# The first batch's later queries: scores from rounded query and key halves instead of full float32

## The chip, the cores and the metric

The kernel runs on one core of one Trainium2 chip. The metric is the device time of one execution in microseconds (us), as the median of several runs; every view of the profile is of one profiled execution of the same program.

## The reference, cut to what matters

```python
scores = 1/sqrt(64) * q @ k.T                     # 8 batches, 8 heads, 576 x 576, head size 64
scores = where(scores >= rowmax(scores) - tau, scores, -1e9)
attn = exp(scores - rowmax(scores)); attn /= attn.sum(-1) + 1e-9
x = (attn @ v) -> (4608, 512)                     # heads side by side, one row per query
h = x @ w_in                                      # (4608, 2048)
out = (s * relu(h)**2 + b) @ w_out                # (4608, 512)
```

The weights come as float64 and are made into float32 on the chip.

## The kernel before, in words

**Tiles.** A tile is 128 queries of one head (or 64 leftover queries of each of two heads, a tail tile) against all 576 keys. For each tile TensorE makes the scores (`s`, line L356, in the PSUM bank `s` or `o`), VectorE takes them out with the row maximum (`sm`, L359), ScalarE makes the exponential (`em`, L365), VectorE masks it and sums it (L368), GpSimd divides (L376), TensorE transposes (`tp` and `tt`, L385 and L386), ScalarE takes the transposes out, and TensorE multiplies with the values (`pv`, L404 or L436). `sm` and `em` have two buffers each.

**Two kinds of attention.** Batch 0 (the first 36 tiles, numbered 0 to 35 here) is plain: its pair of heads lies in one buffer, k in 128 rows (64 of each head), q the same, v beside them (class `Plain`), and the products are in plain float32. From batch 1 on, a head is split (class `Head`): k is loaded twice, into both halves of the 128 partitions of `rk`, and q into `rq`; ScalarE rounds k to the rounded type fp32r (L306), GpSimd makes the rest, k minus its rounded copy (L307), ScalarE rounds q (L314), and VectorE puts the rest of q into the lower 64 rows (L315). One tile's scores are then four fp32r products (two halves of the keys times rounded k and rest of k) over 128 rows, where a plain tile has two float32 products over 64 rows, or over 128 for a tail tile, whose stationary operand `qd` holds the tails of both heads. `rk`, `rq` and `rv` are single buffers.

**Visits.** Each batch is gone through in two halves of queries; a visit is one pair of heads in one half. Batch 0 has tiles 0 to 15 in its first half (four per pair) and tiles 16 to 35 in its second (five per pair, the tail tile third). Tiles 0 to 15 use the banks `s` and `o` in turn, later ones only `s`.

**The feed-forward part** goes over blocks of 256 rows of x: for each of 16 slices f of the 2048 hidden columns, 12 products into bank `h` (L567), relu, square and rounding on ScalarE, a rest `gl` on GpSimd (L577), and 6 products into bank `o` (L583). The weights of a slice are loaded on SyncE's queue (L462 and L465), converted by ScalarE and VectorE (L497 to L508), and stay in the buffer `w0` to `w15`. Block 0 (the first half of batch 0) is worked on while the second half's tiles run, as far as its slices are converted. `xl` (L553) is the rest of its x.

**Borrowed room.** In batch 0 the four pairs lie in buffers that later serve other things: pair 0 in `w15`, pair 1 in `v`, pair 2 in `k`, pair 3 in `e`. A function `split_buffers` hands `e`, `k` and `v` over to the split heads of batch 1.

**The order.** Every operation is entered in a planner (`Plan`) with engine, assumed cost, keys read and written, and a due time; the planner lists them and the result is the fixed order on every engine. Each engine works through its own list in order, so an instruction that waits holds up all behind it. SyncE's list is all the loads.

## Time and profile before

| | |
|---|---|
| runs | 1365.67, 1367.85 and 1368.5 us, median 1367.85 |
| span of the profiled execution | 1365.4 us |
| its own time | not listed by itself; the fastest run stands 0.27 us above the span, the median 2.45 us above |
| TensorE (PE) busy | 1349.2 us, 99% of the span |
| VectorE (DVE) / ScalarE (ACT) / GpSimd (POOL) busy | 1082.1 / 989.4 / 762.3 us |
| granted TensorE clock, mean | 0.997 |
| batch 0's scores on PE | 5.9 us to about 146 us |

How to read it: "busy" is the time in which an engine had an instruction in work; PE matmuls overlap, so their durations are longer than the distance from start to start, and it is the distances that add up to time. In rows of groups the two numbers after the bar are busy us and mean ns of one. In rows of stretches each engine has its busy us and the number of instructions, and then come the granted PE clock, the busy share of the DMA engines and GB/s. In the rows in order of time, the first two columns are the start and the duration in us.

### The profile page before, as it was taken

Reading aid. Unit: us, or ns where it says so; the run is one execution under the profiler, and the core shown is the slowest. Engines: PE = TensorE matmul, PEld = TensorE weight load, DVE = VectorE, ACT = ScalarE, POOL = GpSimd, SP = SyncE. Lnnn points to the kernel's source line nnn. Section 1 sums busy time; section 2 is a strip of 40 time slices with the busy share of each in tenths; the row PEclk is TensorE's granted clock in tenths of the full one; section 3 lists DMA queues with packets and bytes.
Section 4 is the critical chain, followed back from the end, with each engine's and each line's share of the span. In section 5 each row is a group of like instructions: output and inputs, shape, how many; then the busy total and the mean of one; then the engine's idle time right before and its main releaser. Section 6 shows DMA issues by size and latency. Waiting matters only on the chain.

```text
span 1365.4 us, 29419 instructions
## 1 busy us (share of the span) xinstructions
PE 1349.2 (99%) x9369; PEld 1230.8 (90%) x9369; DVE 1082.1 (79%) x3097; ACT 989.4 (72%) x2467; POOL 762.3 (56%) x800
## 2 busy tenths in 40 slices
PE   9899999999999999999999999999999999999998
PEld 6677799998999999999999999999999999999897
DVE  7977789989888888888888888888788888887111
ACT  5787677777777777777777777777777677776443
POOL 2334466665766566655666566655666566664210
PEclk9999999999999999999999999999999999999999
DMA  9530122222222222222222222222222212220000
GB/s 317 206 98 16 37 74 73 85 56 70 77 88 63 62 79 74 77 63 60 71 82 61 72 57 82 72 72 56 61 79 68 75 51 73 67 77 15 17 16 16
DMA packets 94539, 99.59 MB, mean 73 GB/s; under 512 B 34480, under 2 KB 72368, under 8 KB 94384
## 3 DMA queue, kind: packets, MB, share of 16 engines
q1 hardware_dynamic: 94384, 97.71, 24.0%
q8 instruction: 74, 1.21, 0.4%
q14 instruction: 81, 0.66, 0.2%
HBM read 88.21 MB, written 9.44 MB: 72 GB/s over the span
## 4 chain that ended last, share of the span: by engine, by line
PE 93%; DVE 2%; issue 1%; ACT 1%; POOL 0%; DVEq 0%; POOLq 0%; ACTq 0%
PE h L567 30%; PE o L583 29%; PE s L356 12%; PE pv L436 10%; PE tp L385 9%; PE tt L386 2%; PE pv L404 1%; DVE em L368 1%; PE h L519 1%; DVE sm L359 0%; POOL em L376 0%; ACT em L365 0%; DVE e L423 0%; DVE w L508 0%; DVE oo L594 0%
## 5 line engine op out<-in xcount | busy, mean ns | idle before, releaser
L567 PE MATMUL h<-xh,w 128*128 128x256 f32 x2304 | 466.0, 285 | 0.0
L376 POOL TENSOR_SCALAR em<-em,st 128x576 f32<-128x576 f32 x288 | 263.2, 914 | 230.4 <-DVE st L373 137.2
L567 PEld LDWEIGHTS h<-xh,w 128*128 128x128 f32 x2304 | 376.6, 190 | 10.2 <-ACT g L573 1.0
L583 PE MATMUL o<-w,gh 128*128 128x512 f32 x1152 | 371.1, 403 | 0.1
L577 POOL TENSOR_TENSOR gl<-g,gh 128x256 fp32r<-128x256 f32 x272 | 225.7, 830 | 245.8 <-ACT gh L576 94.3
L567 PE MATMUL h<-xl,w 128*128 128x256 f32 x1152 | 325.5, 283 | 0.0
L368 DVE SCALAR_TENSOR_TENSOR em<-sm,st,em 128x577 f32<-128x577 f32 x288 | 273.4, 950 | 13.2 <-ACT em L365 6.6
L365 ACT ACTIVATE em<-sm,st 128x576 f32<-128x576 f32 x288 | 225.1, 781 | 36.2 <-DVE sm L359 18.7
L359 DVE TENSOR_SCALAR_CACHE_REDUCE sm<-s 128x576 f32<-128x576 f32 x280 | 210.9, 753 | 47.3 <-PE s L356 36.4
L573 ACT ACTIVATE g<-h 128x256 f32<-128x256 f32 x288 | 109.9, 381 | 181.6 <-PE h L567 175.3
L583 PE MATMUL o<-w,gl 128*128 128x512 f32 x576 | 226.6, 393 | 0.0
L423 DVE TENSOR_TENSOR e<-tp,e 128x512 fp32r<-128x512 f32 (+1 forms) x280 | 177.7, 635 | 60.2 <-ACT e L420 56.9
L567 PEld LDWEIGHTS h<-xl,w 128*128 128x128 f32 x1152 | 219.2, 190 | 6.2 <-DVE xl L553 0.2
L583 PEld LDWEIGHTS o<-w,gh 128*128 128x128 f32 x1152 | 195.1, 190 | 22.8 <-issue 2.1
L307 POOL TENSOR_TENSOR k<-rk,k 128x576 fp32r<-128x576 f32 x112 | 175.0, 1562 | 59.1 <-ACT k L306 57.0
L420 ACT CAST e<-tp 128x512 fp32r<-128x512 f32 (+1 forms) x280 | 150.7, 538 | 43.7 <-PE tp L385 39.8
L385 PE MATMUL tp<-ident,em 128*128 128x128 f32 x1152 | 174.4, 274 | 3.6 <-POOL em L376 3.2
L356 PE MATMUL s<-k,q 128*128 128x288 f32 x896 | 163.2, 304 | 1.4 <-DVE sm L359 1.4
L385 PEld LDWEIGHTS tp<-ident,em 128*128 128x128 f32 x1152 | 137.7, 140 | 25.5 <-issue 6.1
L436 PE MATMUL pv<-e,v 128*128 128x320 f32 (+1 forms) x1008 | 153.5, 297 | 0.2 <-DVE e L423 0.2
L436 PEld LDWEIGHTS pv<-e,v 128*128 128x128 f32 x1008 | 141.7, 190 | 3.9 <-DVE e L423 1.1
L356 PEld LDWEIGHTS s<-k,q 128*128 128x128 f32 x896 | 132.2, 190 | 7.8 <-DVE sm L359 2.5
(109 smaller groups left out, 1783.3 us busy)
## 6 DMA issues: line engine op xcount, KB each, us to landing
rk<-in_k_dram SPq DMA_DIRECT2D x224, 144.0 KB, 2.7
rv<-in_v_dram SPq DMA_DIRECT2D x112, 128.0 KB, 2.1
rq<-in_q_dram SPq DMA_DIRECT2D x168, 64.0 KB, 2.2
w<-in_moe_w_in_dram SPq DMA_DIRECT2D x16, 512.0 KB, 6.2
w<-in_moe_w_out_dram SPq DMA_DIRECT2D x16, 512.0 KB, 7.0
out_dram<-oo SPq DMA_DIRECT2D x32, 256.0 KB, 2.1
rq<-in_q_dram SPq DMA_DIRECT2D x56, 80.0 KB, 2.4
rv<-in_v_dram SPq DMA_DIRECT2D x224, 16.0 KB, 2.0
```

Of the source, the lines that this page charges most:

```text
L307: pool((1420, 1450), lambda: nc.gpsimd.tensor_tensor(out=klo(), in0=rk, in1=khi().bitcast(F32), op=ALU.subtract), pk + [f"khi{j}"], [f"klo ...
L356: nc.tensor.matmul(ps[:, hf, 0:HS], stat, kk[:, cs], start=(n == 0), stop=(n == len(seq) - 1))
L359: dve((760, 840), lambda: nc.vector.tensor_scalar(out=get()[0][:, 0:S].rearrange("p (a b) -> p a b", a=2), in0=ps[:, :, 0:HS], scalar1=-SC ...
L365: act((690, 785), lambda: nc.scalar.activation(out=get()[1][:, 0:S], in_=get()[0][:, 0:S], func=AF.Exp, bias=st8[:, 0:1], scale=-1.0), [sm ...
L368: dve2((830, 930), lambda: nc.vector.scalar_tensor_tensor(out=get()[1], in0=get()[0], scalar=st8[:, 1:2], in1=get()[1], op0=ALU.is_le, op1 ...
L376: pool((800, 835), lambda: nc.gpsimd.tensor_scalar(out=get()[1][:, 0:S], in0=get()[1][:, 0:S], scalar1=st8[:, 4:5], scalar2=st8[:, 5:6], o ...
L385: nc.tensor.transpose(out=tp[:, t, :], in_=em[:, t * P:(t + 1) * P], identity=ident)
L423: dve((60 + 560 * big, 140 + 560 * big), lambda hi=hi, lo=lo, cs=cs: nc.vector.tensor_tensor(out=lo(), in0=tp[:, :, cs], in1=hi()[:, 0:NQ] ...
L436: nc.tensor.matmul(ps, g.hd.v()[:, kt, :, :], o[:, kt], start=(n == 0), stop=(n == len(seq) - 1))
L567: nc.tensor.matmul(ps, w[:, c, :], x[:, c, :], start=(c == 0 and i == 0), stop=(c == NC - 1 and i == 2))
L577: do((715, 750), lambda: eng.tensor_tensor(out=lo, in0=g, in1=hi.bitcast(F32), op=ALU.subtract), [f"g{k}", f"gh{k}"], [f"gl{k}"], at)
L583: nc.tensor.matmul(bank["o"][:, t, :], a[:, ts_], w, start=(f == 0 and i == 0), stop=(f == NF - 1 and i == 2))
```

## The change

The second half of batch 0 (tiles 16 to 35) takes its scores from split heads: for these visits eight `Head` objects are made beside the `Plain` pairs, loaded into `rk` and `rq` (256 query columns and the 64 of the tail in one transfer) and split as in later batches. The values still come from the plain pair. Three heads' split copies are held at a time: the heads' slots 0 and 1 have k in the buffer `k`, slot 2 has k in the buffer `v`, and all three have q in `v`. For that, pair 1 moves from `v` to `w14`, and pairs 2 and 3 both lie in `e`. The buffers `qd` and their eight small loads go; the tails use `qt`.

```diff
-            self.bi, self.p, self.tag = bi, p_, ("w%d" % (NF - 1), "v", "k", "e")[p_]
+            self.bi, self.p, self.tag = bi, p_, ("w%d" % (NF - 1), "w%d" % (NF - 2), "e", "e")[p_]
...
+            slot = self.i % 3
+            if not self.bi:
+                t = "v" if slot == 2 else "k"
+                hk, lk, qk = (t, "hi", slot), (t, "lo", slot), ("v", "q", slot)
...
+            def early():
+                if "ke" not in lazy:
+                    lazy["ke"], lazy["ve"] = sb("k", [P, 4, S], F32R), sb("v", [P, 2 * S + 3 * NB], F32R)
+                return lazy["ve" if slot == 2 else "ke"]
...
+            act((580, 675), lambda: nc.scalar.copy(out=k_(0), in_=rk), pk, [hk], at)
+            pool((1420, 1450), lambda: nc.gpsimd.tensor_tensor(out=k_(1), in0=rk, in1=k_(0).bitcast(F32), op=ALU.subtract),
+                 pk + [hk], [lk], at)
...
+            if not self.bi:
+                return
...
-        pe(2 if unsplit else 4 * len(ti.heads), HS * (3.7 if unsplit else 1), scores, ti.kq(), [bk], i - SCORES_AHEAD)
+        pe(4 * ti.n_heads or 2, HS * (1 if ti.n_heads else 3.7), scores, ti.kq(), [bk], i - SCORES_AHEAD)
...
-                    ti.st = lambda c=c, r=r: [(A.get()[1][r, c:c + P], A.get()[0][r])]
-                    ti.kq = lambda: A.keys[:2]
+                    if both:
+                        hd, c = both[j], i * P
+                        ti.st = lambda hd=hd, c=c: [(hd.q()[:, c:c + P], kk) for kk in hd.ks()]
+                        ti.kq = lambda hd=hd: hd.kks + hd.kqs
+                    else:
+                        ti.st = lambda c=c, r=r: [(A.get()[1][r, c:c + P], A.get()[0][r])]
+                        ti.kq = lambda: A.keys[:2]
...
-                    ti.st = lambda: [(qd[pair % 2], A.get()[0])]
+                    ti.st = lambda: [(qt[:, j, :], kk) for j, hd in enumerate(both) for kk in hd.ks()]
...
+        both = heads[2 * vi:2 * vi + 2] if vis[0] or vis[2] else None
...
-        for t in qd:
-            nc.gpsimd.memset(t, 0.0)
```

The new costs also make the planner write another order. Three places show it. In all of them a name's number behind the underscore only tells buffers apart, and the line numbers of the changed kernel lie 18 to 26 higher.

On TensorE at the turn from the first to the second half of the queries, before: the scores of tile 17 (plain, from `w15`) stand between the transposes of two tiles.

```order
L385 MATMUL tp_101<-ident_64,em1_82 128x128 x4
L386 MATMUL tt_102<-ident_64,em1_82 64x128
L356 MATMUL s_99<-w15_107 128x288 x2
L385 MATMUL tp_101<-ident_64,em0_80 128x128 x4
L386 MATMUL tt_102<-ident_64,em0_80 64x128
```

At the same turn with the change, the transposes of tiles 14 and 15 stand together, and tile 16's scores (split, slot 2, from `v`) come only behind them.

```order
L403 MATMUL tp_99<-ident_64,em0_78 128x128 x4
L404 MATMUL tt_100<-ident_64,em0_78 64x128
L403 MATMUL tp_99<-ident_64,em1_80 128x128 x4
L404 MATMUL tt_100<-ident_64,em1_80 64x128
L374 MATMUL s_97<-v_461 128x288 x4
```

What moved: before the change five tiles of the second half (16 to 20) have their scores ahead of the first feed-forward product, with it two (16 and 17). The first feed-forward product stands behind 18 tiles' transposes before, behind 16 with the change.

On VectorE, the last instructions before block 0's `xl` (which releases the first feed-forward product), before: they are masks (L368) and maxima (L359) of tiles 16 to 18 and weight conversions (L500, L502).

```order
L368 SCALAR_TENSOR_TENSOR em1_82,st5_78<-sm1_81,st5_78,em1_82 128x577
L500 TENSOR_SCALAR xh1_580<-xh1_580 128x512
L371 RECIPROCAL st5_78<-st5_78 128x1
L373 TENSOR_SCALAR st5_78<-st5_78 128x1
L502 SCALAR_TENSOR_TENSOR xh1_580<-w4_389,xh1_580 128x512
L362 TENSOR_SCALAR st0_73<-st0_73,tau_t_67 128x1
L553 TENSOR_TENSOR xl0_652<-x0_88,xh0_651 128x512
```

With the change the rests of the first split head's q (L331, into `v` and `qt`) stand there, among weight conversions (L518, L520, L526).

```order
L331 TENSOR_TENSOR v_461<-rq_84,v_461 64x256
L331 TENSOR_TENSOR qt_70<-rq_84,qt_70 64x64
L518 TENSOR_SCALAR xh1_606<-xh1_606 128x512
L520 SCALAR_TENSOR_TENSOR xh1_606<-w4_430,xh1_606 128x512
L526 TENSOR_TENSOR w3_617<-xl1_380,w3_617 128x512
L377 TENSOR_SCALAR sm0_77,st4_75<-s_97 128x576
L526 TENSOR_TENSOR w3_617<-xl1_380,w3_617 128x512
L571 TENSOR_TENSOR xl0_639<-x0_86,xh0_638 128x512
```

What moved: ahead of `xl` there are 17 maxima and 16 masks where there were 19 and 18; 26 weight conversions where there were 27 (9, 9 and 8 of the three kinds, where there were 10, 9 and 8); and two subtractions of q are new.

On SyncE's queue behind the last loads of the plain pairs, before: the tails `qd` and then weight slices 4 to 7.

```order
L259 DMA qd0_71<-in_q_dram 64x64 [waits DMAHW2_49,Pool_49]
L259 DMA qd0_71<-in_q_dram 64x64 [waits DMAHW3_49]
L465 DMA w4_389<-in_moe_w_out_dram 128x1024 [waits DMAHW4_49]
L462 DMA w5_463<-in_moe_w_in_dram 128x4x256 [waits DMAHW5_49]
L462 DMA w6_485<-in_moe_w_in_dram 128x4x256 [waits DMAHW6_49]
L462 DMA w7_497<-in_moe_w_in_dram 128x4x256 [waits DMAHW7_49]
```

With the change the loads of `rk` and `rq` stand among the weight slices, and the second and later ones wait for GpSimd, which reads `rk` last.

```order
L276 DMA rk_83<-in_k_dram 64x576 [waits DMAHW2_49]
L480 DMA w4_430<-in_moe_w_in_dram 128x4x256 [waits DMAHW3_49]
L276 DMA rq_84<-in_q_dram 64x320 [waits DMAHW4_49]
L480 DMA w5_457<-in_moe_w_in_dram 128x4x256 [waits DMAHW6_49]
L483 DMA w4_430<-in_moe_w_out_dram 128x1024 [waits DMAHW7_49]
L276 DMA rk_83<-in_k_dram 64x576 [waits DMAHW1_49,DMAHW0_49,Pool_49]
L483 DMA w5_457<-in_moe_w_out_dram 128x1024
L480 DMA w6_523<-in_moe_w_in_dram 128x4x256 [waits DMAHW3_49]
```

What moved: slices 5 to 13 now stand behind loads that wait for a split, and slices 14 and 15 are loaded when pairs 1 and 0 are done with (before, only slice 15 had to wait).

On GpSimd's list, the clearing of `qd` is gone, and `ones` and `qt` are cleared ahead of the identity, not behind it as before; the subtractions of k of the three first split heads stand behind the divisions of tiles 10, 12 and 14.

More of the change, by code (lines that the diff above doesn't have):

```diff
@@ L171, in tile_attention_ffn @@
     qt = const("qt", [P, 2, P], F32R)
-    qd = [const(f"qd{i}", [P, P]) for i in range(2)]
     st = [const(f"st{i}", [P, 8]) for i in range(6)]
@@ L255, in load @@
                     [self.keys[2 + j]], [self.keys[2 + j] + (1,)], at)
-        def load_tail(self, at):
-            for j in range(2):
-                dma(16, lambda j=j: nc.sync.dma_start(
-                    out=qd[self.p % 2][j * D:(j + 1) * D, j * T:(j + 1) * T], in_=qT[self.bi, 2 * self.p + j, :, M:S]),
-                    [f"qd{self.p % 2}"], [(f"qd{self.p % 2}", j)], at)
     class Head:
@@ new lines, in k_, with q_ @@
+            def k_(n):
+                if self.bi:
+                    return lazy["k"][:, 2 * j + n]
+                return early()[:, n * S:(n + 1) * S] if slot == 2 else early()[:, 2 * slot + n]
+            def q_():
+                if self.bi:
+                    return qs[j]
+                early()
+                return lazy["ve"][:, 2 * S + slot * NB:2 * S + (slot + 1) * NB]
+            self.q, self.ks = q_, (lambda: [k_(0), k_(1)])
+            act((580, 675), lambda: nc.scalar.copy(out=k_(0), in_=rk), pk, [hk], at)
@@ L315, in prepare @@
                 dve2(cd, lambda dst=dst, cs=cs: nc.vector.tensor_tensor(
-                    out=dst[D:P], in0=rq[D:P, cs], in1=dst[D:P].bitcast(F32), op=ALU.subtract), pq + [key], [key], at)
+                    out=dst()[D:P], in0=rq[D:P, cs], in1=dst()[D:P].bitcast(F32), op=ALU.subtract), pq + [key], [key], at)
+            if not self.bi:
+                return
             i = self.i % 3
@@ L622, in tile_attention_ffn, with make_tiles @@
             visits += [(bi, p_, 2 * u, 2 * u + 2, (bi > 0 and p_ < NP // 2) == (u == 0)) for p_ in range(NP)]
-    def make_tiles(vis, A, Bh):
+    def make_tiles(vis, A, Bh, both):
         bi, pair, t0, t1, tail = vis
@@ L644, in make_tiles @@
                     ti = Tile_()
-                    ti.st = lambda: [(qd[pair % 2], A.get()[0])]
-                    ti.kq = lambda: [A.keys[0], (f"qd{pair % 2}", 0), (f"qd{pair % 2}", 1)]
+                    ti.st = lambda: [(qt[:, j, :], kk) for j, hd in enumerate(both) for kk in hd.ks()]
+                    ti.kq = lambda: [k for hd in both for k in hd.kks + hd.kts]
+                    ti.n_heads = 2
                     ti.slot, ti.plain = 0, (A, [(0, slice(u_ * T, (u_ + 1) * T)) for u_ in range(2)], xtl,
@@ L667, in half @@
                 ti.kq = lambda hd=hd: hd.kks + hd.kqs
-                ti.heads, ti.plain, ti.blocks = [hd], None, []
+                ti.heads, ti.plain, ti.blocks, ti.n_heads = [hd], None, [], 1
                 ti.parts = [(g, i * P, fl)]
@@ L675, in half @@
                 ti.kq = lambda: A.kks + Bh.kks + A.kts + Bh.kts
-                ti.heads, ti.plain, ti.blocks = [A, Bh], None, []
+                ti.heads, ti.plain, ti.blocks, ti.n_heads = [A, Bh], None, [], 2
                 ti.parts = [(g, NB, slice(0, T))]
@@ L694, in tile_attention_ffn @@
     for vi, vis in enumerate(visits):
-        for ti in make_tiles(vis, *((pairs[vis[1]],) * 2 if vis[0] == 0 else heads[2 * vi:2 * vi + 2])):
+        both = heads[2 * vi:2 * vi + 2] if vis[0] or vis[2] else None
+        for ti in make_tiles(vis, *((pairs[vis[1]],) * 2 if vis[0] == 0 else both), both):
             for hd in ti.heads:
@@ L723, in constants @@
             nc.gpsimd.memset(c[:, S:S + 1], 1e-9)
-    pool((900, 900), constants, [], ["ident", "qd0", "qd1", "sm0", "sm1", "em0", "em1"], -9)
+    pool((900, 900), constants, [], ["ident", "sm0", "sm1", "em0", "em1"], -9)
     for ap, t, k in (s, s_t, "s_"), (b, b_t, "b"):
@@ L736, in tile_attention_ffn @@
         if hd in first:
-            events.append((n_plain - 0.1 if first[hd] < n_plain + 1 else first[hd] - 0.5,
+            events.append((n_plain - 0.1 if n_plain <= first[hd] < n_plain + 1 else first[hd] - 0.5,
                            lambda hd=hd: (hd.load(first[hd] - LOAD_AHEAD), hd.prepare(first[hd] - PREPARE_AHEAD))))
```

32 lines of the change are left out of this document (15 added, 17 removed).

## The prediction

> **What bounds the kernel now.** I read the busy table and the slices first, then the chain of waits, then the first 170 us by stretches.
>
> ```profile
> span 1365.4 us, 29419 instructions
> PE 1349.2 (99%) x9369; PEld 1230.8 (90%) x9369; DVE 1082.1 (79%) x3097; ACT 989.4 (72%) x2467; POOL 762.3 (56%) x800
> PE 93%; DVE 2%; issue 1%; ACT 1%; POOL 0%; DVEq 0%; POOLq 0%; ACTq 0%
> ```
>
> PE is the bound: it is 93% of the chain that ended last. What PE no longer has to do is therefore gained, unless something else then makes it wait. The change lies in the first 164 us, so I cut there.
>
> ```profile
> core 0: us, PE busy (x) PEld busy (x) DVE busy (x) ACT busy (x) POOL busy (x), PEclk, DMA share, GB/s
> 0.00:60.50 60.50, 54.12 (x363) 37.75 (x364) 48.41 (x157) 38.74 (x81) 19.05 (x32) 0.97 0.74 248
> 60.50:163.50 103.00, 100.68 (x714) 78.84 (x712) 81.28 (x212) 74.92 (x172) 43.63 (x42) 0.98 0.24 74
> 180.00:360.00 180.00, 177.55 (x1241) 165.99 (x1240) 161.23 (x461) 135.97 (x348) 116.23 (x118) 1.00 0.25 71
> 240.00:260.00 20.00, 20.00 (x138) 18.57 (x137) 19.09 (x50) 15.40 (x38) 13.75 (x14) 1.00 0.34 102
> 45.00:50.00 5.00, 3.93 (x34) 2.55 (x34) 4.77 (x16) 4.11 (x11) 1.91 (x2) 1.00 0.01 3
> 50.00:55.00 5.00, 4.83 (x30) 3.36 (x30) 5.00 (x17) 3.55 (x7) 1.13 (x2) 0.66 0.00 0
> 60.47 0.69 DVE L553 TENSOR_TENSOR xl<-x,xh 128x512 fp32r<-128x512 f32 x1 [0.48 <-ACT xh L550]
> ```
>
> The first stretch ends where VectorE makes block 0's `xl` (60.47 us); there PE is not the bound. From 45 to 55 us DVE is busy 9.77 of 10 us, PE waits, and the clock falls to 0.66. In the second stretch PE is busy 100.68 of 103 us and DVE 81.28: PE is the bound. That is also so from 180 to 360 us, with DVE at 161.23/180 = 89.6%. So the change must be weighed by DVE's work up to 60.5 us and by PE's work behind it.
>
> **The common point.** In both orders, ahead of the first-layer products of slice 15 PE has done the same list but for the kind of scores: 36 transposed tiles, 20 value products, 90 second-layer products, 39 tiles' scores. In the trace that point is at 163.47 us (row below). Everything behind it is the same work with PE as the bound, so the end moves as this point moves.
>
> **PE's work.** Rows of the chain of waits add up to time, so I take them.
>
> ```profile
> 78.03 0.44 PE tp L385 x4
> 78.46 0.11 PE tt L386
> 78.57 0.97 PE s L356 x4
> 144.57 1.16 PE s L356 x4
> 161.01 1.06 PE s L356 x8
> 163.47 1.63 PE h L567 x12
> 165.64 0.53 PE s L356 x4
> ```
>
> A plain tile's scores take 1.16 us, a plain tail tile's 0.97 (at 78.57), a split tile's 0.53, a split tail tile's 1.06. Sixteen tiles gain 0.63 each, four tails lose 0.09 each: 10.1 - 0.4 = 9.7 us less PE work. The first two plain tiles of the whole kernel run side by side, one per half of the rows (rows at 5.89 and 5.90 us below); in the second half each tile goes through the one bank `s` alone, so no such overlap is given up.
>
> The Trainium skill, page "FP8 and Floating Point Precision", section "TensorE Precision Notes", says that true float32 takes four passes through the array. By that a plain tile would cost twice the split one's two passes, 1.06 us, and a plain tail as much: the saving would be 8.5 us, and my time 1.2 us later. The trace has 1.16 and 0.97, so I stay with the rows.
>
> **The start.**
>
> ```profile
> 0.73 0.20 POOL masks.py:197 MEMSET ident<- 128x128 f32 x1 [0.29 <-POOLq L796]
> 1.81 0.32 POOL L707 MEMSET qt<- 128x256 f32 x1
> 2.18 3.78 PE L713 MATMUL h<-qt,ones 128*128 128x256 f32 x16 [2.18 <-POOL qt L707]
> 5.89 0.85 PE L356 MATMUL s<-w 64*128 64x288 f32 x1
> 5.90 0.85 PE L356 MATMUL o<-w 64*128 64x288 f32 x1
> 1.18 0.41 SPq L247 DMA_DIRECT2D w<-in_q_dram  x1
> w<-in_q_dram SPq DMA_DIRECT2D x1, 256.0 KB, 3.0
> ```
>
> PE waits for `qt`, then runs 16 filler products, and the first scores stand behind them. With the change `ones` and `qt` are cleared where the identity is now (0.73 us, `qt` itself at 1.81), so `qt` is ready about 0.9 us sooner. Ends: 0 (if the first pair's loads then set the start) and -0.9; the last load that the first scores need is issued at 1.18 us and lands 3.0 us later, before 5 us, so I take -0.9.
>
> **First stretch, DVE.** The durations, one execution:
>
> ```profile
> L368 DVE SCALAR_TENSOR_TENSOR em<-sm,st,em 128x577 f32<-128x577 f32 x35 | 30.6, 875 | 3.7 <-ACT em L365 3.5
> L359 DVE TENSOR_SCALAR_CACHE_REDUCE sm<-s 128x576 f32<-128x576 f32 x28 | 21.0, 751 | 20.9 <-PE s L356 13.3 <-PE o L356 7.6
> L500 DVE TENSOR_SCALAR xh<-xh 128x512 int32<-128x512 int32 x16 | 7.5, 472 | 0.4 <-ACT xh L497 0.4
> L362 DVE TENSOR_SCALAR st<-st,tau_t 128x1 f32<-128x1 f32 x35 | 7.2, 206 | 0.0
> L371 DVE RECIPROCAL st<-st 128x1 f32<-128x1 f32 x34 | 5.3, 156 | 0.0
> L373 DVE TENSOR_SCALAR st<-st 128x1 f32<-128x1 f32 x34 | 4.5, 134 | 0.0
> L315 DVE TENSOR_TENSOR q<-rq,q x6: 422/422/846, 146.9 to 193.7; 64x256 fp32r<-64x256 f32 x6
> L315 DVE TENSOR_TENSOR qt<-rq,qt x4: 222/222/224, 149.0 to 181.6; 64x64 fp32r<-64x64 f32 x4
> L307 POOL TENSOR_TENSOR k<-rk,k x22: 1419/1586/2032, 201.5 to 394.8; 128x576 fp32r<-128x576 f32 x22
> ```
>
> One tile is 0.875 + 0.751 + 0.206 + 0.156 + 0.134 = 2.1 us of DVE. Ahead of `xl` two tiles (-4.2) and one conversion (-0.5) go, and the first head's q and tail rests come (0.42 + 0.22): -4.0 us. GpSimd's three subtractions of k are new there; the trace of before has none in this stretch. Bounds: 0 each if DVE works on beside them, 1.59 each if it stands. Nearest row: the worst of six q subtractions took 846 ns where the median is 422, so I take 0.42 each, +1.3. DVE was busy 48.4 of 60.5 us, so I let 80% of the -2.7 count: -2.2 us, ends -4.0 and +0.8. PE's own work there falls by more (below, 5.7 us); the rest becomes waiting, seen in the order as two transposes in a row ahead of tile 16.
>
> **Second stretch, PE.** Before, tiles 21 to 35 remain: 12 x 1.16 + 3 x 0.97 = 16.8 us of scores. With the change tiles 18 to 35: 14 x 0.53 + 4 x 1.06 = 11.7, and two more tiles' transposes, 2 x 0.55: in all -4.0 us. Cover: DVE gets two tiles (4.2), seven heads' q and tails (7 x 0.64 = 4.5), one conversion (0.5) and five subtractions of k beside it (5 x 0.42 = 2.1): 81.3 + 11.3 = 92.6 of 99 us, 93%; PE ran full with DVE at 19.09/20 = 95% from 240 to 260 us. ACT:
>
> ```profile
> L365 ACT ACTIVATE em<-sm,st 128x576 f32<-128x576 f32 x35 | 27.2, 776 | 20.1 <-DVE sm L359 6.4 <-issue 6.0 <-PE tt L386 3.8
> L392 ACT COPY x<-tp 128x512 f32<-128x512 f32 x18 | 10.4, 578 | 2.5 <-PE tp L385 1.2 <-PE pv L404 1.2
> L393 ACT COPY x<-tt 64x128 f32<-64x128 f32 x18 | 4.6, 258 | 0.0
> L306 ACT CAST k<-rk x6: 657/664/676, 135.4 to 190.1; 128x576 fp32r<-128x576 f32 x6
> L314 ACT CAST q<-rq 128x256 fp32r<-128x256 f32 x22 | 8.9, 403 | 0.6 <-PE tp L385 0.6
> 80.00:100.00 20.00, 20.00 (x159) 15.83 (x157) 15.71 (x44) 16.76 (x41) 7.69 (x7) 1.00 0.40 116
> ```
>
> two tiles at 0.776 + 0.578 + 0.258 (3.2), five roundings of k (3.3), seven of q (2.8) and of the four times smaller tails (at most as much again; I take 1.7): 74.9 + 11.0 = 86 of 99 us, 87%; PE ran full with ACT at 16.76/20 = 84% from 80 to 100 us. Both are a little over what the trace shows for long, so I add 0.8 us of waits (ends 0 and 3.5): -3.2 us.
>
> **Loads.** Eight heads bring 16 loads of `rk` and 16 of `rq`, 3.6 MB, and eight of `qd` go. From 45 to 55 us the DMA engines stand idle (0.01 and 0.00), so bytes cost nothing. On SyncE's queue slices 5 to 13 now stand behind loads that wait for GpSimd; but DVE has begun only on the fifth slice when the first stretch ends. Per head, load, rounding and subtraction take some 5 us against 103/8 = 13 us between heads. Nothing added; ends 0 and 2.
>
> **Handover to batch 1.** `k` is now free only behind tile 35's scores: rounding 0.66 and subtraction 1.59 us, against transposes, second-layer and value products of about 4 us that stand between on PE. The next subtraction of k stands ahead of tile 34's division on GpSimd and may hold it 1 to 3 us. Before, this place already cost 2.3 us of idle PE (103 - 100.68, part of it here), so I take no difference, ends -2 and +3.
>
> **Sum.** -0.9 - 2.2 - 3.2 = -6.3 us. The profiled execution's span of 1365.4 becomes 1359.1; the median of the runs stands 2.45 above that span (1367.85), so the median becomes 1361.6 us.
>
> **Rivals.** 0.2%, here 2.7 us, is about what a measurement of this kernel can tell from no change.
>
> - B, PE alone counts: waits don't grow at all. Then -9.7 - 0.9 = -10.6, 1357.2 us. For it: the waits from 45 to 60 us come from DVE work that the new order partly moves behind. Against it: 5.7 us of the PE work fall in the stretch where DVE decides.
> - C, ScalarE takes the gain: 86 us of its work in the second stretch at the 84% that it reached gives 102.4 us against 103, and the first stretch, where it also gets three roundings of k (2.0 us), gains nothing: -0.6 - 0.9 = -1.5, 1366.3 us. For it: every tile's chain passes through ACT. Against it: ACT's idle there is mostly waiting for PE.
> - D, slower: GpSimd's subtractions hold VectorE for their whole length. Then the first stretch has -4.0 + 3 x 1.59 = +0.8, and the second 81.3 + 9.2 + 5 x 1.59 = 98.5 us of DVE work; at the 89.6% of 180 to 360 us that lasts 109.9 us, +6.9. Less 0.9 at the start: +6.8, 1374.7 us. It is slower by over 0.2% from the point where DVE can't be filled over 98.5/105.8 = 93%. Against it: the six q subtractions of the trace have their median at the shortest, 422 ns. The Trainium skill, page "SBUF — State Buffer", section "Who interferes with whom", states such an exclusive lock for a VectorE instruction with two SBUF inputs beside a GpSimd one that reads SBUF; the 846 ns row agrees for single instructions, the medians say that it is rarely met.
>
> **How the numbers follow.** My case 0.60, B 0.10, C 0.20, D 0.10. My case's own range is 1359 to 1365. Faster by over 0.2%: 0.60 + 0.10 = 0.70; within: 0.20; slower: 0.10. The range 1357 to 1368 leaves out D and half of B, and the worst of C.
>
> **What would show it.** The first-layer products of slice 15 start at about 157 us instead of 163.47; the first scores at 5.0; `xl` at about 57.4; a tile's split scores in batch 0 take 0.53 us; PE idle up to 60 us grows by about 2.6 us. It would be wrong if DVE or ACT are full in the second stretch while PE waits, if `sm` or `tp` wait for GpSimd's subtractions, or if further stretches of low clock appear: the one at 50 to 55 us costs 5 x 0.34 = 1.7 us.

## The result, and the profile after

The changed kernel takes 1378.47 us (median of 4 runs, 1377.59 to 1380.23), the kernel before in the same comparison 1368.11 us. The ratio is 1.0080, 95% interval 1.0069 to 1.0092: slower by about 10 us, where I had forecast 1361.6 us. The profiled execution is the slowest of the four (span 1378.4 against 1365.4 us), so differences of spans are up to 3 us larger than those of medians.

The busy table of after; PE's busy time fell by 1.8 us while the span grew by 13.0.

```profile
span 1378.4 us, 29513 instructions
PE 1347.4 (98%) x9385; PEld 1232.5 (89%) x9385; DVE 1103.3 (80%) x3113; ACT 998.7 (72%) x2491; POOL 765.5 (56%) x806
```

The same two stretches as in the prediction, of after (columns: us, then busy us and instructions of PE, weight loads, DVE, ACT and POOL, granted clock, DMA share, GB/s).

```profile
0.00:60.50 60.50, 52.20 (x329) 36.87 (x329) 46.73 (x138) 36.41 (x77) 20.79 (x31) 0.87 0.74 232
60.50:163.50 103.00, 92.32 (x719) 78.19 (x718) 90.25 (x232) 79.99 (x190) 47.56 (x41) 0.98 0.36 111
```

In the second stretch PE is now busy 92.3 of 103 us where it was 100.7, and yet neither DVE (88%) nor ACT (78%) is full. PE waits, and no other engine is the bound: that is the sign of a chain of dependent work, not of a lack of capacity.

The common point of the chain of waits, the first-layer products of slice 15, came at 163.47 us before:

```profile
170.65 1.43 PE h L585 x12
```

So 7.2 us are lost ahead of it and 5.8 behind it. What PE waits for up to the common point, first the three largest of before (times in us: total, how often, longest):

```profile
PE tp L385 <- POOL em L376: 2.8, 2, 1.8
PE h L713 <- POOL qt L707: 2.2, 1, 2.2
PE s L356 <- DVE sm L359: 1.9, 5, 0.6
```

and of after, the four largest:

```profile
PE tp L403 <- POOL em L394: 3.8, 4, 1.4
PE pv L422 <- ACT oo L410: 3.5, 4, 1.0
PE s L374 <- DVE v L331: 3.3, 1, 3.3
PE tp L403 <- ACT xh L515: 2.5, 2, 1.3
```

No single wait took the place of another: there are these four and eight smaller ones, behind three engines. The largest single one is new. It stands at the turn to the second half of the queries, in rows in order of time:

```profile
62.98 0.62 ACT L568 CAST xh<-x 128x512 fp32r<-128x512 f32 x1
...
63.63 0.69 DVE L571 TENSOR_TENSOR xl<-x,xh 128x512 fp32r<-128x512 f32 x1 [0.82 <-ACT xh L568]
...
64.74 0.39 ACT L330 CAST v<-rq 128x256 fp32r<-128x256 f32 x1
...
65.55 0.42 DVE L331 TENSOR_TENSOR v<-rq,v 64x256 fp32r<-64x256 f32 x1
...
66.02 1.33 PE L374 MATMUL s<-k,v 128*128 128x288 f32 x4 [3.28 <-DVE v L331]
...
67.15 0.41 PE L585 MATMUL h<-xh,w 128*128 128x256 f32 x1
```

`xl` is ready at 64.3 us, but PE's list has tile 17's split scores ahead of the first feed-forward product, and those need the rest of q, whose rounding stands on ACT behind the last pieces of x, an exponential and a weight conversion. PE stands from 62.7 to 66.0 us and then works at half clock.

The accounting used below is worked out from each trace: the time in which no matmul runs (idle), half of the time in which matmuls run while the granted clock is 0.5 (lost to the clock), and the rest (work), up to the common point, and the time from there to the end of the last matmul (behind).

| | idle | lost to clock | work | behind |
|---|---|---|---|---|
| before | 8.7 | 3.4 | 151.2 | 1197.3 |
| after | 20.6 | 8.0 | 141.9 | 1203.4 |
| after - before | +11.9 | +4.6 | -9.3 | +6.1 |

### The profile page after: what moved, and what is told of

It reads as the page before. It is cut to its first block, busy times and chain, and to the rows that moved or that the text cites. A ratio compares the mean times of both kernels' runs of the same rounds, so it can differ in the third digit from the quotient of the medians.

```text
span 1378.4 us, 29513 instructions
## 1 busy us (share of the span) xinstructions
PE 1347.4 (98%) x9385; PEld 1232.5 (89%) x9385; DVE 1103.3 (80%) x3113; ACT 998.7 (72%) x2491; POOL 765.5 (56%) x806
## 4 chain that ended last, share of the span: by engine, by line
PE 84%; DVE 2%; ACT 1%; issue 1%; DMA 0%; POOL 0%; DVEq 0%; SPq 0%; ACTq 0%; POOLq 0%
PE h L585 27%; PE o L601 27%; PE s L374 10%; PE pv L454 10%; PE tp L403 8%; PE tt L404 2%; DVE em L386 1%; DVE e L441 0%; DVE sm L377 0%; DMA rk<-in_k_dram 0%; ACT e L438 0%; DVE q L331 0%; PE pv L422 0%; DVE e L443 0%; ACT g L591 0%
## 5 line engine op out<-in xcount | busy, mean ns | idle before, releaser
L386 DVE SCALAR_TENSOR_TENSOR em<-sm,st,em 128x577 f32<-128x577 f32 x288 | 282.0, 979 | 18.6 <-ACT em L383 11.1
L323 POOL TENSOR_TENSOR k<-rk,k 128x576 fp32r<-128x576 f32 x117 | 179.4, 1533 | 82.4 <-ACT k L322 80.2
```

The source lines that it names most:

```text
L323: pool((1420, 1450), lambda: nc.gpsimd.tensor_tensor(out=k_(1), in0=rk, in1=k_(0).bitcast(F32), op=ALU.subtract), pk + [hk], [lk], at)
L386: dve2((830, 930), lambda: nc.vector.scalar_tensor_tensor(out=get()[1], in0=get()[0], scalar=st8[:, 1:2], in1=get()[1], op0=ALU.is_le, op1 ...
```

## The experiments

A kernel's order of instructions is written by the planner from assumed costs; I call the result the list. My first theories were parts of the split work (rival D's lock, the queue, the low clock). The last ones are about the list itself. Where an edit is shown in part, `...` marks what is left out. "Over before" is (ratio - 1) x 1367.5 us, with the interval of the ratio; each ratio is against runs of before on the same chip.

| kernel | median us | ratio, interval | over before | idle / clock / work / behind |
|---|---|---|---|---|
| after | 1378.47 | 1.0080, 1.0069-1.0092 | +10.9 | 20.6 / 8.0 / 141.9 / 1203.4 |
| e1_no_k_rest | 1374.35 | 1.0055, 1.0037-1.0072 | +7.5 | 19.1 / 5.0 / 141.0 / 1202.9 |
| e2_no_q_rest | 1376.67 | 1.0064, 1.0046-1.0082 | +8.8 | 19.4 / 8.1 / 141.7 / 1202.7 |
| e3_plain_scores | 1384.99 | 1.0130, 1.0109-1.0151 | +17.8 | 14.3 / 12.8 / 152.3 / 1202.9 |
| e5_one_head | 1375.03 | 1.0065, 1.0043-1.0086 | +8.9 | 17.2 / 9.9 / 142.2 / 1202.9 |
| p1_side_by_side | 1373.65 | 1.0044, 1.0029-1.0059 | +6.0 | 19.1 / 10.0 / 138.0 / 1200.1 |
| e4_early_k | 1387.51 | 1.0130, 1.0097-1.0163 | +17.8 | 21.3 / 17.2 / 139.7 / 1202.3 |
| v1_tile16_ahead | 1376.53 | 1.0069, 1.0054-1.0084 | +9.4 | 22.1 / 3.4 / 141.3 / 1202.1 |
| f1_fillers | 1384.64 | 1.0127, 1.0112-1.0142 | +17.4 | 14.4 / 1.7 / 159.7 / 1201.9 |
| s1_old_tail | 1378.08 | 1.0077, 1.0061-1.0094 | +10.5 | 21.5 / 6.3 / 141.9 / 1202.3 |
| h1_hold | 1366.63 | 1.0002, 0.9990-1.0013 | +0.3 | 8.9 / 3.0 / 149.3 / 1197.3 |
| n1_before_51 | 1369.87 | 1.0012, 1.0003-1.0021 | +1.6 | 8.8 / 1.7 / 150.7 / 1200.4 |
| n2_after_51 | 1386.28 | 1.0140, 1.0114-1.0166 | +19.1 | 23.9 / 9.0 / 141.8 / 1202.3 |
| g1_half_scores | 1360.22 | 0.9948, 0.9933-0.9963 | -7.1 | 9.2 / 1.7 / 144.4 / 1198.6 |
| g2_half_scores_list | 1376.40 | 1.0064, 1.0044-1.0083 | +8.8 | 11.4 / 7.8 / 142.8 / 1207.9 |
| p2_list_for_one | 1368.47 | 1.0010, 1.0001-1.0020 | +1.4 | 14.4 / 3.4 / 136.5 / 1207.2 |
| o2_old_order | 1394.26 | 1.0200, 1.0172-1.0229 | +27.4 | 31.8 / 17.2 / 142.1 / 1197.5 |
| o3_old_list | 1368.35 | 1.0011, 0.9999-1.0024 | +1.5 | 16.6 / 5.9 / 140.1 / 1197.7 |
| o4_searched | 1359.08 | 0.9940, 0.9927-0.9953 | -8.2 | 13.5 / 1.6 / 139.7 / 1198.1 |

Each split is of one profiled execution, and that can lie up to 4 us from the median of its kernel (e3's and e5's are their slowest, h1's and v1's their fastest). n1 has the list of before up to 250 us, and its execution reached the common point 2.3 us sooner; so differences in the split below that say little. In five lists other products stand ahead of the point: in p1 20 value and 8 score products have moved behind it, in p2 6 second-layer products more, by the rows of the chain some 2.5 and 3.8 us of work; in n2, o4 and h1 at most 1.4 us.

### Parts of the split work, in after's list

**e1_no_k_rest.** GpSimd's rests of k are left out for batch 0; the scores there multiply with the rounded k twice, so PE has as much to do.

```diff
-            self.q, self.ks = q_, (lambda: [k_(0), k_(1)])
+            self.q, self.ks = q_, (lambda: [k_(0), k_(1 if self.bi else 0)])
...
+            def rest():
+                if self.bi:
+                    nc.gpsimd.tensor_tensor(out=k_(1), in0=rk, in1=k_(0).bitcast(F32), op=ALU.subtract)
+            pool((1420, 1450), rest, pk + [hk], [lk], at)
```

> The changed kernel in its own order, with GpSimd's eight subtractions of k in batch 0 left out (the scores there multiply with the rounded k twice, so TensorE does as much as with the rest). Queue theory (the one raw buffer rk and in-order queues: a late rest on GpSimd holds SyncE's weight loads and the divisions behind it): the divisions are no longer held by 1.6 us each at the turn, but the loads still wait for ScalarE's rounding, which ends at 39.8 us where the rest ended at 41.3: 3 to 5 us faster than the changed kernel, 1373 to 1376. Contention theory (VectorE is the bound because GpSimd's rests slow it): the q rests fall back to 422 ns and the 6 us longer conversions with them, some 10 us faster, 1366 to 1369.

Measured: 3.4 us of the 10.9 go (0.5 to 6.3 by the two intervals). In the profiled executions the loss to the clock falls by 3.0 us and the idle time by 1.5; the time behind stays. The run takes away three things at once: the rests themselves, the waits for them, and the lock of rival D. So in this list the lock is worth, by the medians, a third of the loss at most.

**e2_no_q_rest.** VectorE's rests of q are left out for batch 0.

```diff
-                dve2(cd, lambda dst=dst, cs=cs: nc.vector.tensor_tensor(
+                dve2(cd, lambda dst=dst, cs=cs: None if not self.bi else nc.vector.tensor_tensor(
```

> The changed kernel in its own order, with VectorE's rests of q in batch 0 left out (both halves of the partitions hold the rounded q; 16 instructions, 10.6 us of VectorE in the trace of the changed kernel before the common point). Contention or VectorE-work theory: VectorE is nearly full from 103 to 151 us, so 5 to 10 us come back: 1368 to 1373. Queue theory: only the waits of TensorE for these rests at tiles 16 and 17 go (3.3 us in the waits): 1375 to 1377.

Measured: 2 us less, with overlapping intervals. The rests of q are not the main cause.

**e3_plain_scores.** All the splits stay, but the sixteen full tiles take plain scores.

```diff
-                        ti.st = lambda hd=hd, c=c: [(hd.q()[:, c:c + P], kk) for kk in hd.ks()]
+                        cc = t0 * P + i * P
+                        ti.st = lambda cc=cc, r=r: [(A.get()[1][r, cc:cc + P], A.get()[0][r])]
```

> The changed kernel in its own order with all its loads and splits, but the 16 full tiles of the second half take their scores from the plain pair, as before the change; nobody reads the split copies of those tiles. TensorE gets 16 x 0.63 = 10.1 us more work. If TensorE were still the bound there: 10 us slower than the changed kernel, 1388. If VectorE and the queues set the time up to the common point, as both theories say, most of it is hidden: 0 to 4 us slower, 1378 to 1382; the part that shows is what the change really gains on TensorE.

Measured: 6.9 us slower than after. PE's work is 10.4 us more, its idle time 6.3 less. In after's list the faster scores are thus worth 7 us, two thirds of the work that they save: the premise of the change holds.

**e5_one_head.** Only the first split head is loaded and split; the other seven heads' loads, roundings and rests are left out, and their tiles use the first head's copies.

```diff
+            skip, real = not self.bi and self.i > 8, 2 if not self.bi else slot
...
-            act((580, 675), lambda: nc.scalar.copy(out=k_(0), in_=rk), pk, [hk], at)
+            act((580, 675), lambda: None if skip else nc.scalar.copy(out=k_(0), in_=rk), pk, [hk], at)
...
```

> The changed kernel in its own order, but only the first split head of batch 0 is loaded and split; loads, roundings and rests of the other seven are left out, and all scores of the second half multiply with the first head's copies (as many products as with the change). What stays is TensorE's gain, the rooms and the planner's new order. Work theory (the idle time of TensorE up to the common point, 20.6 us against 8.7 before, comes from the splits' work and the waits for it): it falls back to about 10 us and the kernel comes out at 1362 to 1367. Order theory (the idle time comes from the new list, with the transposes of tiles 14 and 15 in a row and tile 16's scores late): 17 us or more stay, 1371 to 1376.

Measured: 2 us less, with overlapping intervals. Seven eighths of the split work and of the new loads on SyncE's queue can vanish and the time hardly moves, as long as the list stays. So most of the loss does not go with the amount of split work.

**p1_side_by_side.** The planner never lets two of its "port" operations run together. Here it is told that the new heads' rests of k and q may (`last` takes the mark off the operation just entered); the work is that of after, in another list.

```diff
+            if not self.bi:
+                plan.last()
...
```

> The changed kernel with all its work; only the planner is told that the rests of k and q of the eight new heads may run beside VectorE's and GpSimd's other work. (It assumes that a GpSimd instruction and a VectorE instruction of certain kinds, rests, masks and conversions among them, never run at the same time, and so makes room for 8 rests of k and 16 of q in its list.) List theory (the list is stretched for that assumption, and the chip mostly runs them side by side): the common point comes near 157 us instead of 170.5, TensorE's idle time up to it falls from 20.6 to some 12 us, 1360 to 1368. Lock theory (GpSimd's rests really stop VectorE, so the assumption is right): nothing is gained, 1374 to 1382.

Measured: 4.9 us better than after with all the work in it, as large a step as any removal of work above. The time lies between the two ranges expected.

### Repairs at single places of after's list

**e4_early_k.** Roundings and rests of k of the first three split heads are moved to earlier places.

```diff
...
+    work = plan.moved([(('khi', 8, 0), ('exp', 8, 0)), (('klo', 8, 0), ('div', 8, 0)),
+        (('khi', 9, 0), ('prelu', (3, 1), 0)), (('klo', 9, 0), ('div', 11, 0)), ...])
```

> The changed kernel, all work done; only the rounding of k (ScalarE) and its rest (GpSimd) of the first three split heads stand earlier in their engines' orders: the rests ahead of the divisions of tiles 8, 11 and 13, where they stood behind those of tiles 10, 12 and 14. Queue theory: the second head's loads of k leave SyncE's queue at about 32 us instead of 41.3, the weight slices behind them too, no division is held at the turn, and the conversions move back out of the middle: 7 to 10 us faster, 1368 to 1371. Contention theory: the same instructions beside the same ones elsewhere, at most 2 us: 1376 to 1378.

Measured: 7 us slower than after, against my expectation. Moved ahead, the rounding now waits for its load, with ScalarE's whole queue behind it:

```profile
29.65 0.67 ACT L360 CAST v<-rk 128x576 fp32r<-128x576 f32 x1 [2.44 <-DMA rk<-in_k_dram]
```

The tiles come late, and the clock stays at half for 20.5 us, as the stretch behind it shows:

```profile
35.50:56.00 20.50, 19.73 (x92) 12.62 (x90) 11.87 (x38) 9.20 (x21) 6.90 (x7) 0.50 0.56 180
```

**v1_tile16_ahead.** Tile 16's splits and scores are put ahead of tile 13's transposes.

```diff
...
+    work = plan.moved([(('khi', 8, 0), ('prelu', (2, 1), 0)), (('klo', 8, 0), ('div', 9, 0)), ...
+        (('s', 16, 0), ('tp', 13, 0)), (('sm', 16, 0), ('shr', (2, 1), 0))])
```

> The changed kernel, all work done, in its own order but for tile 16: the splits of its head stand earlier (rounding of k behind the loads, its rest ahead of tile 9's division, q behind tile 8's copies), and its scores stand ahead of the transposes of tile 13 instead of behind those of tile 15. Turn theory (from 44 to 59 us TensorE has nothing but transposes and value products that wait for each other, because tile 16's scores stand last): the first feed-forward product comes 4 to 6 us earlier and less time is spent at half clock, 1371 to 1375. If the turn is set by VectorE's and ScalarE's work and not by where the scores stand: 1377 to 1381.

Measured: in the profiled execution the first feed-forward product comes at 63.1 us instead of 67.2, at a better clock, but over before the two differ by 1.5 us only, with overlapping intervals. From slice 7's products to the common point it takes 66.7 us, as after does (66.8; before 60.0): mending the turn leaves the second stretch as it was.

**f1_fillers.** 156 products that nobody needs are put on PE ahead of the transposes and scores of tiles 8 to 17.

```diff
...
+            nc.tensor.matmul(bank["h"][:, 0:P], ones, ones, start=True, stop=True)
...
```

> The changed kernel in its own order, with 156 filler products (128 columns each, into the bank h that is free until the first feed-forward product) put on TensorE ahead of the transposes of tiles 8 to 15, four value products and the scores of tiles 16 and 17. Clock theory (the idle TensorE at the turn drops to half clock for 20.5 us, and the half clock itself lengthens the chain from tile to tile): the granted clock stays at 1 from 40 to 60 us (0.62 in the changed kernel), the common point comes 4 to 7 us earlier, 1371 to 1375. Queue theory (TensorE waits for the divisions and splits whatever its clock): the fillers only fill gaps, 1376 to 1380.

Measured: 6.5 us slower than after. The clock is full at the turn, where after has 0.62 from 40 to 60 us:

```profile
40.00:60.00 20.00, 19.23 (x172) 16.24 (x170) 14.54 (x39) 11.05 (x26) 8.99 (x8) 1.00 0.57 188
```

But the fillers take 17.8 us of PE to save 6.3 us of clock and 6.2 of idle time. And with the clock full up to the first feed-forward product, the stretch from slice 7 to the common point still takes 68.3 us: the low clock at the turn is not what makes that stretch long.

**s1_old_tail.** After's list up to the common point, the list of the kernel before behind it.

```diff
...
+    cut, r = rank[891], N
+    for n in table:
+        if rank[n] > cut:
+            rank[n] = r = r + 1
...
```

> The changed kernel in its own order up to the first-layer products of slice 15 (the common point, 170.5 us there), and behind it in the order that the kernel before has there, held as a table. All work is done. Order theory (the planner writes the whole list anew, and what it writes behind the common point is some 5.5 us worse by chance; the profiles have 1197.6 us behind the point against 1191.7): 5 us faster than the changed kernel, 1372 to 1375. If the 5.9 us come from the state in which the changed kernel leaves the first batch (late weights, late handover), or from the spread of single profiles, the time stays at 1377 to 1379.

Measured: no gain in all. From the next first-layer products on, the old list takes 1191.4 us where after's takes 1196.6, but 4.3 us are lost where the two lists meet, in rows of waits from 168 to 178 us:

```profile
POOL v L544 <- ACT v L543: 7.8, 1, 7.8
ACT v L543 <- DMA rv<-in_v_dram: 3.3, 1, 3.3
PE tp L609 <- POOL em L600: 3.2, 1, 3.2
```

A subtraction of v stands on GpSimd for a load and holds a division that PE waits for. So 5 of the 6 us lost behind the common point belong to the order of the work there, and an old list can't be put behind a new one without a price at the seam.

### The list

**h1_hold.** The kernel before, with the rooms `k` and `v` marked as in use up to tile 35.

```diff
+                    ti.kq = lambda: A.keys[:2] + ([("k", "hold"), ("v", "hold")] if u else [])
```

> The kernel before with plain scores, all its own work and its own rooms; only the planner is told that the rooms k and v are in use until tile 35's scores, as they are with the change, so the first splits of k and v of batch 1 stand behind that point. It has the list of the changed kernel for the last 1100 us or so. Handover theory (the held rooms push batch 1's first splits together, and the list behind follows from that): the 5 to 6 us that the changed kernel loses behind the common point appear here, 1371 to 1375. If they come from the splits of batch 0 alone: 1366 to 1369.

Measured: no difference. The held rooms cost nothing, as predicted. This is a new list too, on every engine from the first 12 us on, and it loses nothing, so a new list is not slow by itself. From 346 us on it has the same order on PE, DVE, ACT and GpSimd as after has from 360 us on, and the two take 1017.4 and 1017.9 us from there: what after loses against h1, it loses ahead of that.

**n1_before_51 and n2_after_51.** In both kernels the planner's assumed delay of a handover between engines is 51 instead of 50 ns. The instructions are the same, the list is another: n1's differs from before's only from 250 to 859 us, n2's from after's from the first 12 us on.

```diff
-    HANDOVER = 50
+    HANDOVER = 51
```

> The kernel before, with one assumption of its planner changed by a fiftieth (a result reaches another engine after 51 ns instead of 50), so that the planner writes another list for the same work. Order theory: the list of the kernel before is a lucky one, and a new list is 3 to 8 us slower with nothing else changed: 1371 to 1376. If lists hardly matter: 1366 to 1369.

> The changed kernel with the same small change of the planner's assumption (51 ns instead of 50). Order theory: several us to either side of the changed kernel, 1370 to 1386, with the part behind the common point off by some us. If lists hardly matter: 1377 to 1380.

Measured: n1 is 1.6 us slower than before, less than expected, and n2 8.2 us slower than after (3 to 13 by the two intervals; its four runs spread over 7.5 us). One nanosecond in a table moves the changed kernel by nearly as much as the change moved the kernel.

**g1_half_scores and g2_half_scores_list.** In the kernel before, the sixteen full tiles of the second half make only one half of their scores, which takes 16 x 0.58 = 9.3 us of work from PE by the rows (6.8 by the accounting) and adds nothing. g1 keeps the list of before, g2 tells the planner the lower cost (the last line).

```diff
+        short = 16 <= i < n_plain and (i - 16) % 5 != 2
-            for hf in range(2):
+            for hf in range(1 if short else 2):
...
+        pe(2 if unsplit else 4 * len(ti.heads), HS * (1.85 if short else 3.7 if unsplit else 1), scores, ti.kq(), [bk], i - SCORES_AHEAD)
```

> The kernel before in its own order; the 16 full tiles of the second half make the scores of only the first 288 keys (one of two products; the other half of the bank keeps what an earlier tile left). That takes 16 x 0.58 = 9.3 us from TensorE, as much as the change does, and adds nothing anywhere. If TensorE bounds that stretch as the prediction says: 8 to 10 us faster than before, 1357 to 1360. If the other engines' chain of each tile is close behind TensorE: the gain turns into idle time of TensorE, 2 to 6 us faster, 1361 to 1366.

> The same half scores, and the planner knows their cost, so that it writes another list. List theory (a new list loses what the tuned one had): slower than with the old list, 1363 to 1370. If the planner uses the room: 1355 to 1360.

Measured: the same instructions are 7.1 us faster than before in the old list and 8.8 us slower than before in the new one. The second stretch of g1 and then of g2:

```profile
60.50:163.50 103.00, 99.99 (x739) 79.92 (x739) 89.24 (x230) 80.77 (x188) 50.86 (x45) 1.00 0.24 76
```

```profile
60.50:163.50 103.00, 98.95 (x695) 78.32 (x696) 82.65 (x214) 75.26 (x173) 43.89 (x42) 0.93 0.23 69
```

Less work, a planner that knows it, and some 16 us (12 to 19 by the two intervals) lost by the list alone, with none of the splits in it. g1 also settles a rival: DVE is busy 89.24 us in it, nearly as much as after's 90.25, and PE still ran 99.99 of 103 us. So it is not DVE's load that makes PE wait in after.

**p2_list_for_one.** The instructions of e5, and the planner is told what is left out.

```diff
...
+            if skip:
+                plan.last((0.1, 0.1))
...
```

> The same instructions as in the kernel with only the first split head (loads, roundings and rests of the other seven left out, all scores of the second half with the first head's copies), but the planner knows that the seven are left out, so its list is made for what runs. That kernel, in the changed kernel's list, took 1375.0 us. List theory: 1358 to 1366, since the idle time came from a list with room for eight splits. If a list with the borrowed rooms and the new handover is slow whatever it has room for: 1371 to 1376.

Measured: 7.5 us better than e5 with the same instructions, if not as fast as I expected and still no faster than before. Together with e5: what the seven other heads cost is not their work but the list that is made to fit them in.

**o2_old_order.** All the work of after; the instructions that before also has in its order, the new ones put in between by hand.

```diff
...
+    for r, n in enumerate(n for n in table if n not in NEW):
+        rank[n] = r
...
```

> The changed kernel with all its work, in the order of the kernel before, held as a table; the loads and splits of the eight new heads are put into it by hand (each head's rest of k and of q 5 to 20 us ahead of its first tile, by the trace of the kernel before), and the first loads and splits of batch 1 are moved behind tile 35, whose scores hold the rooms until then. Order theory: TensorE's work falls by 9 us, its idle time stays near the 8.7 us of before plus 2 to 4 at the handover to batch 1: 1360 to 1365. Work theory (the splits cost what they save, in whatever order): 1370 to 1378.

Measured: the worst of all. My places were bad (PE waited 12.6 us for GpSimd's divisions, in five places), and tile 17's scores slipped on PE, so this run told nothing about the old list.

**o3_old_list.** The same idea done properly: every old instruction in the order of before on its engine (batch 1's first splits give way), and the places of the new ones found by a search over a simple model of the queues. The order is a table.

```diff
...
-    work = plan.run()
...
+    work = [plan.ops[n][3] for n in struct.unpack("<%dH" % (len(table) // 2), table)]
```

> All the work of the change, with every instruction that the kernel before also has in the order of the kernel before on each engine, and the new loads, roundings and rests put in between (batch 1's first splits, of heads 16 to 18, give way to them). List theory (the loss is the planner's newly written list): 1364 to 1370 us, about the time of before. Split-work theory (the splits cost what the fast scores save, in whatever order): 1374 to 1380 us, about the time of after.

Measured: 1368.35 us, the time of before within the interval, 9.4 us better than after, with all of after's work. Behind the common point it takes 1197.7 us, as before does (1197.3). What PE waits for up to the common point, the two largest:

```profile
PE tp L590 <- POOL em L581: 5.2, 5, 2.5
PE s L561 <- DVE sm L564: 5.0, 4, 2.6
```

**o4_searched.** The same work; the search also moves old instructions of the first 190 us. The edit is that of o3 with another table.

> The same work as after, with an order of the first 190 us that was searched starting from the order of the kernel before, old instructions moved too. List theory: 1357 to 1365 us, faster than before. Split-work theory: 1374 to 1380 us.

Measured: 1359.08 us (1358.39 to 1359.43), ratio 0.9940, interval 0.9927 to 0.9953: faster than both kernels. It reaches the common point at 154.8 us. PE alone in its two stretches:

```profile
0.00:60.50 60.50, 52.65 (x377) 0.97 0.82 244
60.50:163.50 103.00, 97.32 (x773) 1.00 0.37 113
```

PE does 377 and 773 matmuls there where after does 329 and 719, at a clock of 0.97 and 1.00 where after has 0.87 and 0.98. Not tried: whether the same search would also speed up the kernel before. So o4 shows what the change's work can do in a list that suits it, not that the change alone is worth 8 us.

## Why the prediction was wrong

The chain of runs adds up: before 0, g1 -7.1 (PE's saving, old list), o3 +1.5 (the loads, splits and rooms put into the old list: +8.6), after +10.9 (the planner's list instead: +9.4). The searched list takes 19.1 us off after. The loss against before is thus the list; the split work in the old list merely eats what the fast scores save. The planner's own lists scatter: with the work of before its three lie within 4 us (h1, before, n1), with the work of after all three are slower than before, by 6, 11 and 19 us (p1, after, n2). Only lists that the planner did not write (o3, o4) reach the time of before or beat it.

- **The saving on PE was right.** Predicted 9.7 us less work up to the common point, measured 9.3. A split tile was to take 0.53 us; after's rows give 0.54 from its scores to the next product:

```profile
89.90 0.70 PE L374 MATMUL s<-v 128*128 128x288 f32 x4
90.44 0.27 PE L585 MATMUL h<-xh,w 128*128 128x256 f32 x1
```

- **The start was right.** The first scores come at 4.96 us where they came at 5.89, as forecast.
- **The first stretch was wrong.** It was to end 3.1 us sooner (-0.9 - 2.2); the first feed-forward product went from 63.46 to 67.15 us, 3.7 later, and `xl` came at 63.63 instead of 57.4 us. The step that failed is the -2.2: DVE was to have 2.7 us less to do ahead of `xl`, 80% of that was to count, and "the rest becomes waiting". The stretch of after up to its `xl`:

```profile
0.00:63.63 63.63, 54.45 (x349) 38.58 (x349) 48.70 (x142) 38.61 (x82) 20.79 (x31) 0.87 0.75 235
```

  DVE was busy 48.7 us where it was 48.4, and it stood 14.9 us where it stood 12.1. The term in it that was far too small is GpSimd's rests of k, put at 0.42 us each on DVE (+1.3). In e1's execution, without them, `xl` comes at 57.45 us; in e5's, with the first head's rest alone, at 63.27, though DVE is busy only 46.6 us there; in v1's, with that rest and tile 16's scores moved ahead, at 59.68. So the runs, one execution of each, point to the first rest and to what waits for it, not to DVE's sum. It stands on GpSimd ahead of a division that PE's transposes wait for:

```profile
39.89 1.40 POOL L323 TENSOR_TENSOR v<-rk,v 128x576 fp32r<-128x576 f32 x1 [2.27 <-ACT v L322]
41.28 1.82 POOL L394 TENSOR_SCALAR em<-em,st 128x576 f32<-128x576 f32 x1
...
43.16 0.66 PE L403 MATMUL tp<-ident,em 128*128 128x128 f32 x4 [0.72 <-POOL em L394]
```

  From 44.96 us PE then has half the clock. Both are signs of being wrong that the prediction names: `tp` waits behind a subtraction of k, and further stretches of low clock appear. And `xl` was not the end of the stretch: tile 17's rest of q was, behind the chain ACT - DVE - PE shown above. That chain was to be read in PE's list, which has tile 17's split scores ahead of the first product; I had quoted the place and counted only instructions.
- **The second stretch was wrong.** Predicted -3.2; from the first product to the common point it takes 103.5 us where it took 100.0. From `xl`, where the prediction cut, to the common point:

```profile
63.63:170.65 107.02, 95.62 (x744) 80.91 (x745) 94.38 (x242) 82.17 (x195) 52.36 (x46) 0.98 0.33 103
```

  The sums of DVE (92.6 us predicted, 94.4 measured) and of ACT (86 and 82.2) were near enough; the step "I add 0.8 us of waits" failed: PE stood 11.4 us here where it stood 2.3. Up to the common point PE's idle time and its loss to the clock grew by 16.5 us, where the prediction had 2.6 in the first stretch and 0.8 in the second.
- **"Everything behind it is the same work with PE as the bound, so the end moves as this point moves" was wrong** by 6 us. It is the same work, but the planner wrote it anew up to about 1250 us; with the old list behind the common point (o3) the 6 us are gone.
- **Handover, bytes and the loads' queue were right** at nothing: h1 shows no cost of the held rooms, e5 only 2 us for seven eighths of the loads and splits together, with overlapping intervals.
- **Rival D** (1374.7 us) was the nearest in time, but in this list its mechanism carries, by the medians, a third at most: e1 gives back 3.4 us. p1 gives back 4.9, but by another list. Rival C fell: ACT is at 78% in the second stretch. B's premise, that only PE's sum counts, holds only as long as the list stays (g1).

What stays open: which places of after's list cost how much. e4 made it worse, v1 and s1 mended one place and little of it reached the end; no small set of moves was found, only whole lists.

## What to carry to other kernels

Where a planner writes the order from costs, a change is two changes: the work, and a new list from the first instruction to the last. Price the work by sums, but measure the list by itself: a null change of one cost (here 1 ns moved the median of a kernel by 8 us), and the new work put into the old list. And where the bound engine waits while no other engine is full, busy sums say little; follow the two or three chains in which a new operation stands between the old ones, above all where it is placed ahead of the product that starts the next stage.

## What the runs showed of the hardware

**The clock.** In these traces the granted clock changes only at the borders of pieces of 3.41 us; in after it is low for five of them in a row and later for one. Stretches of that length of after, with PE alone (us, busy us and matmuls, granted clock):

```profile
41.55:44.96 3.41, 2.02 (x11) 1.00 0.59 159
44.96:48.37 3.41, 3.06 (x21) 0.50 1.02 358
...
58.61:62.03 3.42, 3.42 (x23) 0.50 0.93 254
62.03:65.44 3.41, 0.71 (x10) 1.00 0.96 326
65.44:68.85 3.41, 2.83 (x12) 0.50 0.87 294
68.85:72.27 3.42, 3.42 (x30) 1.00 0.56 184
```

A piece in which PE was busy for 2.02 of 3.41 us was followed by half clock, and 17.07 us passed at half until a full piece ended it. The Trainium skill, page "TensorE: Matmul & The Clock Gate", Part 1, section "What's actually happening", gives a free-running window of 3413 ns, with half clock after an idle window; the length agrees, but here a window that was 59% busy was enough. No sharp threshold can be read: at half clock 2.83 us of work brought the full clock back, and 3.06 us did not. The prediction had put nothing for more of it: the loss to the clock is 8.0 us in after, 17.2 in e4 and o2.

**DVE beside GpSimd.** A conversion that takes 0.69 us alone took 1.89 beside a rest of k on GpSimd, and a rest of q 0.86 instead of 0.42 beside a division:

```profile
51.78 0.82 POOL L394 TENSOR_SCALAR em<-em,st 128x576 f32<-128x576 f32 x1 [2.94 <-DVE st L391]
...
55.13 1.45 POOL L323 TENSOR_TENSOR k<-rk,k 128x576 fp32r<-128x576 f32 x1 [2.52 <-ACT k L322]
55.24 1.89 DVE L526 TENSOR_TENSOR w<-xh,w 128x512 fp32r<-128x512 f32 x1
...
56.57 1.78 POOL L394 TENSOR_SCALAR em<-em,st 128x576 f32<-128x576 f32 x1
...
57.76 0.86 DVE L331 TENSOR_TENSOR v<-rq,v 64x256 fp32r<-64x256 f32 x1
...
62.13 0.69 DVE L526 TENSOR_TENSOR w<-xl,w 128x512 fp32r<-128x512 f32 x1
```

The conversion takes 1.20 us longer beside a rest of 1.45 us, so it stood for most of the other's length, as rival D supposed; the division is stretched as well (1.78 us, where the first row's takes 0.82). But leaving the rests of k out (e1) or planning them otherwise (p1) gave back only 3 to 5 us.
